# A convolution's stationary operand laid out by channel quartets, and half of x staged in VectorE's buffers

## The chip, the cores and the metric

The kernel runs on one core of one Trainium2 chip. The metric is the device time of one execution in microseconds (us). A core has a matrix engine (TensorE, "PE" in the profile; its weight loads are listed apart as "PEld"), VectorE ("DVE"), ScalarE ("ACT"), GpSimd ("POOL"), a queue engine ("SP") and 16 DMA engines. Each engine works through its own instruction queue in order and waits on semaphores for the others. On-chip tensors have 128 partitions; PS is the accumulation memory, eight banks of 128 x 512 numbers.

## The reference

Two independent halves, whose results lie side by side in the output. Half A is multi-head attention over 2048 positions with 32 heads of 16 channels. Half B is a gated long convolution over 512 channels:

```python
qkv = (x @ wqkv) ...                       # A: x is 2048 x 512
scores = einsum("bhqd,bhkd->bhqk", q, k) * Dh ** -0.5
a = (softmax(scores) @ v) @ wo
k_shift = sum of 4 shifted copies of k, each times shift_k[:, tap]     # B
kv = k_shift * v
y = causal convolution of kv with ssm_k (one filter of 2048 taps per channel) + kv * ssm_D
out = concatenate([a, q * y], -1)
```

## The kernel before, in words

*Attention.* x is transposed on TensorE (`turn_first` L663, `turn_x` L478) into xT; projections give KTo, QT and VAF. The scores come in blocks of 128 keys x 512 queries for one head (2048 blocks, L779, four heads side by side in row strips). Two or three blocks form a step T; ACT exponentiates two or three blocks in one instruction (L786, 726 of them) into PT. From step 82 on one block of many steps goes to DVE instead: a conversion of PS into the integer buffer EI (L805), a linear piece on GpSimd (L284), two polynomial steps (L814) and a last one into PTD (L815). 256 blocks go that way. Probabilities times values accumulate in PS (L854); DVE transposes and normalizes each finished group (L880 to L895); the output projection is L928 and L940.

*Convolution.* For half B, chunks of 256 positions of k (four shifted copies) and v are loaded; DVE multiplies and adds the taps (L588, L592) and multiplies by v into KV (L608, two instructions for each of eight chunks, `kv_chunk`). KV holds the gated values as [position in tile, time tile, channel], 16 tiles of 512 channels. The filters are written to memory reversed and read back, channel by channel, as Toeplitz tiles of 128 x 2048 into the ring WR (14 slots, `load_wr`, 512 loads of 512 KB on the SP queue). For each quartet of channels `conv_lags` (L980) runs 16 lags; lag n loads 16 - n columns of KV of one channel as weights and streams 128 columns of WR, four channels in four column strips of the array. A finished group of four quartets is copied by DVE (L996), transposed on PE (L1007), multiplied by q (L1022) and stored.

*KV is used twice.* Before the gated values exist, the 16 tiles of x are loaded into KV (`load_x`, L383) and transposed from there; each L608 waits for the semaphore of the transposes issued last (`h_xt`).

*Order.* A planner in the kernel's own code emits every engine's queue while the program is built. It keeps a clock for each engine from costs written beside each operation (460 ns for L608, 692 ns for most DVE operations); `dve_job` puts a DVE operation on a list with a due time, `commit_one` picks the next one, and PE's steps, convolution bursts (`emit_lags`), zero-weight filler matmuls (`keep_active`, L1104) and loads are placed by the same clock. A changed cost may thus change the order of everything behind it.

Of the kernel before, what the change touches and what calls it, by code (L numbers as in the profile page):

```python
# [6 lines left out]
ALU = mybir.AluOpType  # L7
BF16 = mybir.dt.bfloat16
# [16 lines left out]
C = 512  # L25
NB = S // 128
# [145 lines left out]
def bass_concat_heads__mha_block__ssm_conv_h3__prompt_kernel(  # L172
# [12 lines left out]
    x2, q2, k2, v2, out2 = A_x[0], B_q[0], B_k[0], B_v[0], out[0]  # L185
# [4 lines left out]
    def enter(cm):  # L190
        ctxs.append(cm)
        return cm.__enter__()
# [4 lines left out]
    def sb(name, shape, dt=BF16):  # L197
        return enter(nc.sbuf_tensor(name, shape, dt))
# [5 lines left out]
    VAF = sb("VAF", [128, KT, VROW])  # L204
    PT = sb("PT", [128, R_PT, 3 * QB])
    WR = sb("WR", [128, R_W, S])
    KV = sb("KV", [128, NB, C])
    QN = sb("QN", [128, NB, 256])
    WQ = sb("WQ", [128, 4, D])
    MSK = sb("MSK", [128, 2, 4], FP32)  # L210
# [7 lines left out]
    IDN = sb("IDN", [128, 128])  # L218
    SHK = sb("SHK", [128, 4, 4])
    PTD = sb("PTD", [128, 4, QB])  # L220
    EI = sb("EI", [128, 4, QB], INT32)
    EM = sb("EM", [128, 2, QB], FP32)
    ZER = sb("ZER", [128, 128])
    JNK = sb("JNK", [128, 2], FP32)
    WK = WKV[:, 0, :, :]
    WV = WKV[:, 1, :, :]
# [22 lines left out]
    def job(fn, deps, cost, due, then=None):  # L249
        j = Job(fn, deps, cost, due, then)  # L250
        jobs.append(j)
        return j
# [81 lines left out]
    def pe_op(fn, deps, mms):  # L334
        advance(pe.t)
        return pe.op(fn, [force(d) for d in deps], cost=Mm(*mms))

    def dve_op(fn, deps=(), cost=692.0):
        return dve.op(fn, [force(d) for d in deps], cost=cost)
# [3 lines left out]
    def dve_job(fn, deps, cost=692.0, slack=900.0, then=None, two=False):  # L343
        if dyn[0]:
            j = job(fn, deps, cost, pe.t + slack + cost, then)
            j.two = two
            return j
        h = dve_op(fn, deps, cost)
        if then:
            then(h)  # L350
        return h

    def full(n, k):
        return [("full", 0, n)] * k

    def dma(eng, dsem, outp, inp, deps=(), transpose=False):
        h = dsem.add()

        def fn(e):
            f = e.dma_start_transpose if transpose else e.dma_start  # L360
            f(outp, inp).then_inc(dsem.sem, 16)  # L361
        eng.op(fn, deps, inc=False)
        return h
# [16 lines left out]
    d_x0 = DmaSem(sem("d_xa"))  # L380

    def load_x(eng, ds, t0, t1):
        return dma(eng, ds, KV[:, t0:t1, :], x2[t0 * 128:t1 * 128, :].rearrange("(t p) d -> p t d", p=128))  # L383

    def landing(h, us):
        Eng.at[(id(h[0]), h[1])] = 1000.0 * us
# [52 lines left out]

    h_j = dve.op(lambda e: e.memset(JNK[:], 0.0))  # L440
    h_w0 = dve.op(lambda e: e.memset(PT[:, 0, 0:512], 0.0))
# [13 lines left out]
    h_vaf1 = pool.op(lambda e: e.memset(VAF[:, :, H * VW:VROW], 1.0))  # L455
    h_zer = pool.op(lambda e: e.memset(ZER[:, :], 0.0))
    h_kz0 = pool.op(lambda e: e.memset(KZS[:, :, S:S + PAD], 0.0))
# [3 lines left out]

    act.op(lambda e: e.activation(JNK[:, 1:2], JNK[:, 0:1], ACT.Exp), [h_j], inc=False)

# [4 lines left out]
    h_xt = [None]  # L468

    def turn_x(sc, cp, bank, eng):  # L470
        pbf = PS[:, bank, :].bitcast(BF16)

        def fn(e):
            ins = None
            for i in range(2):
                for t in range(4):
                    c = 2 * cp + i
                    ins = e.transpose(pbf[:, 512 * i + 128 * t:512 * i + 128 * t + 128],  # L478
                                      KV[:, 4 * sc + t, 128 * c:128 * c + 128], IDN[:, :])
            return ins  # L480
        h = pe_op(fn, [h_xn[sc], h_idn, bank_free[bank]], full(128, 8))
        h_xt[0] = h
        dst = xT[:, 2 * cp:2 * cp + 2, sc * 512:(sc + 1) * 512]
        src = pbf.rearrange("p (i s) -> p i s", i=2)
        if eng is act:
            hh = act.op(lambda e: e.activation(dst, src, ACT.Copy), [h], cost=940.0)
        else:
            hh = dve_job(lambda e: e.tensor_copy(dst, src), [h])
        bank_free[bank] = hh
        h_x.setdefault(sc, []).append(hh)  # L490
# [85 lines left out]
            evac_unit(u, bank, pe_unit(u, bank), eng)  # L576


    kv_pieces = []
    h_kvc = [None]  # L580

    def kv_chunk(j):
        b = kvbuf[kv_buf[j]]
        st = {}

        def tap(m):
            in1 = TB[:, m:m + 1, :].broadcast_to([128, 2, D])
            st[m] = dve_job(lambda e: e.tensor_tensor(b[m], b[m], in1, ALU.mult),  # L588
                            [h_kv[(j, 0)], h_kv[(j, 1)], h_tb[m]], 750.0, 3000.0)

        def add(m):
            st["a"] = dve_job(lambda e: e.tensor_tensor(b[3], b[3], b[m], ALU.add), [st[m], st[3], st.get("a")], 750.0, 3500.0)  # L592

        def last():
            def then(h):
                h_kvfree[j] = h
                nxt = {4: 1, 3: None, 2: 0}.get(j, j - 3)
                if nxt is not None and nxt >= 0:
                    load_kv(nxt)
                for d in {6: (0, 1), 5: (2, 3), 4: (4, 11), 3: (8, 9, 12, 13), 1: (5, 6, 7)}.get(j, ()):  # L600
                    load_wr(d, [h])
                if j == 5:
                    load_qn(0, [h_kzt[0]], 4, NB)
                    line[0] += 5000.0
                elif j == 0:
                    start_conv(h)
            for i in range(2):
                dve_job(lambda e, i=i: e.tensor_tensor(KV[:, NB - 1 - 2 * j - i, :], b[3][:, i, :], b[4][:, i, :], ALU.mult),  # L608
                        [st["a"], h_xt[0]], 460.0, 4000.0 + i, then if i else None)
        return [lambda m=m: tap(m) for m in (3, 2)] + [lambda: add(2), lambda: tap(1), lambda: add(1),  # L610
                                                       lambda: tap(0), lambda: add(0), last]

# [44 lines left out]
    def turn_first(cs, t0, dep):  # L657
        def fn(e):
            ins = None
            for c in cs:  # L660
                for t in range(t0, t0 + 2):
                    pbf = PS[:, first_bank[c], :].bitcast(BF16)
                    ins = e.transpose(pbf[:, 128 * t:128 * t + 128],  # L663
                                      KV[:, t, 128 * c:128 * c + 128], IDN[:, :])
            return ins
        return pe_op(fn, [dep, h_idn], full(128, 2 * len(cs)))

# [53 lines left out]
    def pvb(n):  # L721
        return BGB if n == 1 else PVB
# [246 lines left out]
    def conv_lags(qd, n0, n1):  # L969
        kk = qd % 8  # L970
        deps = [h_wr[4 * qd + c] for c in range(4)] + [h_kvc[0]]
        if kk % 4 == 0 and n0 == 0:
            deps.append(bank_free[BGB])

        def fn(e):
            ins = None
            for n in range(n0, n1):
                for c in range(4):
                    d = 4 * qd + c
                    ins = e.matmul(PS[32 * c:32 * c + NB - n, BGB, 128 * (kk % 4):128 * (kk % 4) + 128],  # L980
                                   lhsT=KV[:, n:NB, d],
                                   rhs=WR[:, d % R_W, 128 * (NB - 1 - n):128 * (NB - n)],
                                   start=(n == 0), stop=(n == NB - 1), tile_position=(0, 32 * c))
            return ins
        h = pe_op(fn, deps, [("col", c, 128) for n in range(n0, n1) for c in range(4)])
        if n1 == NB:
            for c in range(4):
                h_wrfree[4 * qd + c] = h
                if 4 * qd + c + R_W < C:
                    load_wr(4 * qd + c + R_W)  # L990
            if kk % 4 == 3:
                half = kk // 4
                src = PS[:, BGB, :]
                src = bass.AP(tensor=src.tensor, offset=PS[:, BGB, 127:128].offset,
                              ap=[src.ap[0], [128, 4], [-1, 128]])
                bank_free[BGB] = dve_job(lambda e: e.tensor_copy(YB[:, half, :].rearrange("p (k i) -> p k i", k=4), src),  # L996
                                         [h, (lambda: h_yb.get(qd // 8 - 1, WAIT)) if qd >= 8 else None])
                h_yb_in[qd // 4] = bank_free[BGB]
        return h
# [94 lines left out]
    def keep_active(T, limit):  # L1094
        n = open_group[0]
        for _ in range(3):
# [4 lines left out]
            def fn(e):  # L1101
                ins = None
                for s in range(4):
                    ins = e.matmul(PS[32 * s:32 * s + 32, pvb(n), :], lhsT=ZER[:, 0:32],  # L1104
                                   rhs=IDN[:, :].rearrange("p (a f) -> p a f", a=1).broadcast_to([128, 4, 128]),
# [61 lines left out]
    def keep_zero(e):  # L1167
        return e.matmul(PS[:, BGB, :], lhsT=ZER[:, :], rhs=IDN[:, :].rearrange("p (a f) -> p a f", a=1).broadcast_to([128, 4, 128]),
                        start=False, stop=False)
# [93 lines left out]
    while flow["NT"] is None or T < flow["NT"] + 2:  # L1263
# [12 lines left out]
        if T < T_DYN:  # L1276
            if early and early[0][0] <= T:
                t = max(max(Mm.tile), pe.t)
# [79 lines left out]
```

## Time and profile before

| | us |
|---|---|
| median of three runs | 864.66 (862.82 to 866.16) |
| the profiled execution | 861.98 |
| its span, first to last instruction | 860.2 |
| ScalarE busy | 835.9 |
| VectorE busy | 817.0 |
| TensorE busy | 726.8 |
| GpSimd busy | 295.2 |

A row of a group reads: line, engine, operation, output<-inputs, shape and count, then total busy time in us and the mean of one in ns, then the idle time of the engine just before these instructions and what ended it. A row of the waits reads: who waited <- for whom, us in total, times, longest. A row of a window gives the busy time of each engine in that stretch, with counts in brackets, TensorE's granted clock (1.00 is full), the DMA engines' busy share and GB/s. A row of the timeline gives start, duration, instruction and count, and in brackets the idle time ahead of it.

### The profile page before, as it was taken

How to read it: one execution, taken by the hardware profiler on the slowest of the kernel's cores; microseconds unless marked ns; L12 is line 12 of the kernel's file. 1: busy time of each engine (PE TensorE's matmuls, PEld its weight loads, DVE VectorE, ACT ScalarE, POOL GpSimd, SP SyncE). 2: the span in 40 equal slices, each digit the busy share in tenths (PEclk: the TensorE clock that was granted, in tenths of full speed). 3: DMA queues.
4: the chain of work that ended last, by engine and by line, in shares of the span. 5: the costliest groups of instructions: out<-in, count | busy, mean ns of one | idle time of the engine just before them, and what ended most of it. 6: DMA issues, size and time to landing. Idle time of an engine off the chain costs nothing.

```text
span 860.2 us, 30079 instructions
## 1 busy us (share of the span) xinstructions
PE 726.8 (84%) x13244; PEld 325.6 (38%) x13244; DVE 817.0 (95%) x1342; ACT 835.9 (97%) x732; POOL 295.2 (34%) x317
## 2 busy tenths in 40 slices
PE   8989988888788888888888888888888887888787
PEld 3322343434344434343434334343333333434332
DVE  3888999999999999999999999999999999999995
ACT  6999999999999999999999999999999999999997
POOL 3233132333333333333334433333333333333331
PEclk9999999999999999999999999999999999999999
DMA  9877599999999999999999999999999999999922
GB/s 314 300 242 261 168 362 330 367 402 380 372 369 354 406 363 386 380 370 377 369 350 366 345 393 403 387 376 372 374 377 327 349 386 393 377 366 393 383 88 74
DMA packets 88435, 295.69 MB, mean 344 GB/s; under 512 B 11125, under 2 KB 19314, under 8 KB 87922
## 3 DMA queue, kind: packets, MB, share of 16 engines
q1 hardware_dynamic: 82386, 280.00, 87.4%
q0 software_dynamic: 3776, 12.58, 4.3%
q8 instruction: 105, 1.72, 0.8%
q10 hardware_dynamic: 2144, 1.18, 0.5%
q14 instruction: 24, 0.20, 0.1%
HBM read 287.31 MB, written 6.42 MB: 341 GB/s over the span
## 4 chain that ended last, share of the span: by engine, by line
ACT 57%; DVE 30%; PE 10%; issue 2%; DMA 1%; POOL 0%; ACTq 0%; DVEq 0%
ACT PT L786 57%; DVE EM L814 6%; DVE PTD L815 6%; DVE EI L805 6%; DVE WKV L814 6%; PE PS L779 3%; PE PS L854 2%; PE PS L514 1%; PE PS L507 1%; DVE YB L996 1%; DMA WKV<-in_A_wqkv_dram 1%; PE PS L980 1%; DVE DT L880 1%; PE PS L500 1%; DVE OUTA L940 1%
## 5 line engine op out<-in xcount | busy, mean ns | idle before, releaser
L786 ACT ACTIVATE PT<-PS 128x1536 bf16<-128x1536 f32 (+1 forms) x726 | 832.3, 1362 | 12.8 <-PE PS L779 11.3
L779 PE MATMUL PS<-QT,KTo 32*128 32x512 bf16 x2048 | 285.5, 385 | 116.4 <-ACT PT L786 93.2
L980 PE MATMUL PS<-WR,KV 128*10 128x128 bf16 (+15 forms) x8192 | 255.9, 223 | 4.0 <-issue 2.7
L980 PEld LDWEIGHTS PS<-WR,KV 128*6 128x6 bf16 (+15 forms) x8192 | 184.5, 107 | 75.5 <-issue 41.7
L284 POOL TENSOR_SCALAR EM<-EI 128x512 f32<-128x512 uint16 x128 | 127.9, 999 | 224.1 <-DVE WKV L814 107.0
L284 POOL TENSOR_SCALAR WKV<-EI 128x512 f32<-128x512 uint16 x128 | 129.5, 1012 | 218.9 <-DVE EM L814 83.5
L854 PE MATMUL PS<-PT,VAF 128*32 128x512 bf16 x1792 | 186.3, 392 | 1.4 <-issue 0.5
L805 DVE TENSOR_SCALAR EI<-PS 128x512 int32<-128x512 f32 x256 | 182.2, 712 | 1.7 <-PE PS L779 1.3
L814 DVE SCALAR_TENSOR_TENSOR EM<-EM 128x512 f32<-128x512 f32 x256 | 181.0, 725 | 1.5 <-POOL EM L284 1.4
L814 DVE SCALAR_TENSOR_TENSOR WKV<-WKV 128x512 f32<-128x512 f32 x256 | 181.3, 727 | 0.9 <-POOL WKV L284 0.7
L779 PEld LDWEIGHTS PS<-QT,KTo 32*128 32x128 bf16 x2048 | 72.6, 91 | 271.8 <-ACT PT L786 222.1
L815 DVE SCALAR_TENSOR_TENSOR PTD<-EI,EM 128x512 uint16<-128x512 int32 x128 | 92.3, 722 | 0.4
L815 DVE SCALAR_TENSOR_TENSOR PTD<-EI,WKV 128x512 uint16<-128x512 int32 x128 | 91.5, 716 | 0.6
L854 PEld LDWEIGHTS PS<-PT,VAF 128*32 128x32 bf16 x1792 | 46.9, 93 | 105.5 <-issue 98.2
L854 PE MATMUL PS<-PTD,VAF 128*32 128x512 bf16 x256 | 78.3, 387 | 4.4 <-DVE PTD L815 3.8
L1104 PE MATMUL PS<-IDN,ZER 128*32 128x512 bf16 x440 | 46.7, 380 | 0.3 <-issue 0.3
L854 PEld LDWEIGHTS PS<-PTD,VAF 128*32 128x32 bf16 x256 | 19.6, 94 | 26.1 <-DVE PTD L815 17.4
L880 DVE STREAM_TRANSPOSE DT<-PS 128x512 f32<-128x512 f32 x31 | 23.6, 760 | 6.1 <-PE PS L854 5.8
L996 DVE CAST YB<-PS 128x512 bf16<-128x512 f32 x32 | 22.0, 687 | 0.2
L535 DVE TENSOR_TENSOR QT<-PS,MSK 128x1024 bf16<-128x1024 f32 x15 | 18.5, 1230 | 3.4 <-PE PS L500 3.3
L361 POOL DMA_DIRECT2D WR<-in_B_k_dram x15 | 11.0, 737 | 30.1 <-DVE KV L608 21.0
L361 POOL DMA_DIRECT2D out_dram<-OUTA x12 | 7.1, 590 | 38.2 <-DVE OUTA L940 38.2
(77 smaller groups left out, 312.8 us busy)
## 6 DMA issues: line engine op xcount, KB each, us to landing
WR<-kz_scratch SPq DMA_DIRECT2D x512, 512.0 KB, 7.7
WR<-in_B_k_dram POOLq DMA_DIRECT2D x15, 256.0 KB, 7.0
kz_scratch<-WR SPq DMA_DIRECT2D x1, 2176.0 KB, 8.6
out_dram<-QN POOLq DMA_DIRECT2D x2, 1024.0 KB, 8.5
QT<-in_B_k_dram POOLq DMA_DIRECT2D x7, 256.0 KB, 8.6
KV<-in_A_x_dram SPq DMA_DIRECT2D x3, 512.0 KB, 9.0
out_dram<-OUTA POOLq DMA_DIRECT2D x12, 128.0 KB, 5.6
WR<-in_B_v_dram SPq DMA_DIRECT2D x5, 256.0 KB, 4.8
```

What stands on the lines that cost most here:

```text
L284: q.h = pool.op(lambda e: e.tensor_scalar(UB[m % len(UB)], f, PA, PB, ALU.mult, ALU.add), [h, fx.h, free], cost=Beside((h[0], h[1] + 1)))
L535: hh = dve_job(lambda e: e.tensor_tensor(QT[:, qb % 2, 2 * o:2 * o + 2, :], src, MSK[:, :, 0:1].broadcast_to([128, 2, QB]), ALU.mult), [h, ...
L779: ins = e.matmul(PS[:, bank, :], lhsT=KTo[32 * s:32 * s + 32, g // 2, kt * 128:(kt + 1) * 128], rhs=QT[32 * s:32 * s + 32, qb % 2, g, :], ...
L786: h_exp[T] = act.op(lambda e: e.activation(PT[:, T % R_PT, 0:n * QB], PS[:, banks[0]:banks[0] + n, :].rearrange("p b f -> p (b f)"), ACT.E ...
L805: h_fix[i] = job(lambda e: e.tensor_scalar(ei, PS[:, bank, :], FIX_LO, FIX_ADD, ALU.max, ALU.add), [h, h_pair.get(i - 4)], 692.0, end)
L814: js.append(job(lambda e, c=c: e.scalar_tensor_tensor(u, u, c, u, ALU.add, ALU.mult), [js[-1]], 693.0, due + 700.0 * (len(js) - 3)))
L815: js.append(job(lambda e: e.scalar_tensor_tensor(PTD[:, i % 4, :].bitcast(UINT16), ei, 2.0 ** -9, u, ALU.mult, ALU.add), [js[2], (lambda: ...
L854: ins = e.matmul(PS[32 * s:32 * s + 32, pvb(qb * NG + g), :], lhsT=VAF[:, kt, h * VW:h * VW + 32], rhs=rhs, start=first[b], stop=last[b], ...
L880: h_t = dve_job(lambda e: e.transpose(out=dt, in_=PS[:, pvb(n), :]), [h, h_mult.get(n - 2 if n == 2 else n - 1) if n != 1 else None], 717. ...
L980: ins = e.matmul(PS[32 * c:32 * c + NB - n, BGB, 128 * (kk % 4):128 * (kk % 4) + 128], lhsT=KV[:, n:NB, d], rhs=WR[:, d % R_W, 128 * (NB - ...
L996: bank_free[BGB] = dve_job(lambda e: e.tensor_copy(YB[:, half, :].rearrange("p (k i) -> p k i", k=4), src), [h, (lambda: h_yb.get(qd // 8 ...
L1104: ins = e.matmul(PS[32 * s:32 * s + 32, pvb(n), :], lhsT=ZER[:, 0:32], rhs=IDN[:, :].rearrange("p (a f) -> p a f", a=1).broadcast_to([128, ...
```

## The change

KV is laid out as [position in tile, channel quartet, time tile, four channels]. A weight load of lag n then reads its 16 - n columns 4 elements (8 bytes) apart, where they were 512 elements (1,024 bytes) apart. The gated multiply writes 128 runs of four channels, 64 elements apart, where it wrote 512 channels in a row; its inputs are as before. A time tile of KV now lies across the whole buffer, so a gated tile would overwrite x everywhere: x keeps the first half of the buffer for its tiles 0 to 7 (XL, a flat view of KV), and its tiles 8 to 15 are loaded into EI, seen as bfloat16 (XH). The planner's cost of the multiply goes from 460 to 700 ns.

```diff
-    KV = sb("KV", [128, NB, C])
+    KV = sb("KV", [128, C // 4, NB, 4])
...
+    XL = KV[:, :, :, :].rearrange("p q t r -> p (q t r)").rearrange("p (t d) -> p t d", t=NB)
+    XH = EI[:, :, :].rearrange("p i f -> p (i f)").bitcast(BF16).rearrange("p (t d) -> p t d", t=8)
+
+    def xn(t):
+        return XL[:, t, :] if t < 8 else XH[:, t - 8, :]
...
     def load_x(eng, ds, t0, t1):
-        return dma(eng, ds, KV[:, t0:t1, :], x2[t0 * 128:t1 * 128, :].rearrange("(t p) d -> p t d", p=128))
+        return dma(eng, ds, XL[:, t0:t1, :] if t0 < 8 else XH[:, t0 - 8:t1 - 8, :], x2[t0 * 128:t1 * 128, :].rearrange("(t p) d -> p t d", p=128))
...
-                                      KV[:, 4 * sc + t, 128 * c:128 * c + 128], IDN[:, :])
+                                      xn(4 * sc + t)[:, 128 * c:128 * c + 128], IDN[:, :])
...
+    def quads(ap):
+        return ap.rearrange("p (q r) -> p q r", r=4)
+
...
-                dve_job(lambda e, i=i: e.tensor_tensor(KV[:, NB - 1 - 2 * j - i, :], b[3][:, i, :], b[4][:, i, :], ALU.mult),
-                        [st["a"], h_xt[0]], 460.0, 4000.0 + i, then if i else None)
+                dve_job(lambda e, i=i: e.tensor_tensor(KV[:, :, NB - 1 - 2 * j - i, :], quads(b[3][:, i, :]), quads(b[4][:, i, :]), ALU.mult),
+                        [st["a"], h_xt[0]], 700.0, 4000.0 + i, then if i else None)
...
-                                      KV[:, t, 128 * c:128 * c + 128], IDN[:, :])
+                                      xn(t)[:, 128 * c:128 * c + 128], IDN[:, :])
...
-                                   lhsT=KV[:, n:NB, d],
+                                   lhsT=KV[:, qd, n:NB, c],
```

## The prediction

> **What bounds the kernel now.** I read the page's busy times first, then the chain of work that ended last, then the groups with shapes kept apart, the waits, and two windows. ScalarE (ACT) and VectorE (DVE) are both nearly full:
>
> ```profile
> span 860.2 us, 30079 instructions
> PE 726.8 (84%) x13244; PEld 325.6 (38%) x13244; DVE 817.0 (95%) x1342; ACT 835.9 (97%) x732; POOL 295.2 (34%) x317
> ...
> ACT 57%; DVE 30%; PE 10%; issue 2%; DMA 1%; POOL 0%; ACTq 0%; DVEq 0%
> ```
>
> ```profile
> L786 ACT ACTIVATE PT<-PS 128x1536 bf16<-128x1536 f32 x340 | 528.0, 1608 | 5.0 <-PE PS L779 4.3
> L786 ACT ACTIVATE PT<-PS 128x1024 bf16<-128x1024 f32 x386 | 428.0, 1145 | 7.8 <-PE PS L779 7.1
> ```
>
> ```profile
> PEld PS L779 <- ACT PT L786: 222.1, 461, 1.2
> ACT PT L786 <- PE PS L779: 11.3, 25, 1.2
> SPq L361 <- PE PS L980: 294.4, 79, 7.5
> ```
>
> ```profile
> core 0: us, PE busy (x) PEld busy (x) DVE busy (x) ACT busy (x) POOL busy (x), PEclk, DMA share, GB/s
> 36.00:98.00 62.00, 56.18 (x370) 16.65 (x368) 54.90 (x96) 59.59 (x60) 15.86 (x20) 0.97 0.71 241
> 100.00:845.00 745.00, 625.78 (x12588) 292.39 (x12584) 732.84 (x1196) 736.96 (x631) 266.92 (x269) 1.00 0.97 361
> ```
>
> ACT runs the 726 exponentials almost without a break: 835.9 of 860.2 us, 24.3 us idle in all. Between 100 and 845 us, where the convolution runs, it is idle for 745.00 - 736.96 = 8.0 us and DVE for 12.2 us. The waits point one way: TensorE's loads for the scores stand 222.1 us behind ACT, while ACT stands 11.3 us behind TensorE (PE). So PE has room, ACT and DVE do not, and the queue that loads the Toeplitz tiles waits for PE to free them (294.4 us), not PE for it. Any change on PE alone can win at most those few microseconds of ACT's idle time.
>
> **The change, part by part.** The instruction order of both programs says that the counts stay: 740 instructions on ACT, 1344 on DVE, 544 on SP, 321 on POOL; 256 tiles are exponentiated on DVE in both. PE issues 12 filler matmuls fewer (428 for 440). Up to the first convolution lag PE's order is the same.
>
> *The gated multiply* (16 instructions) writes runs of four channels, 128 bytes apart, in place of 512 in a row. Its rows, and the nearest ones:
>
> ```profile
> L608 DVE TENSOR_TENSOR KV<-WR 128x512 bf16<-128x512 bf16 x10 | 3.8, 418 | 0.1
> L608 DVE TENSOR_TENSOR KV<-QT,QN 128x512 bf16<-128x512 bf16 x6 | 2.3, 417 | 0.0
> L1022 DVE TENSOR_TENSOR QN<-PS,QN 128x512 bf16<-128x512 bf16 x16 | 11.2, 700 | 0.2 <-PE PS L1007 0.2
> L551 DVE CAST VAF<-PS 128x512 bf16<-128x512 f32 x16 | 11.0, 690 | 8.1 <-PE PS L514 8.0
> L545 DVE CAST KTo<-PS 128x512 bf16<-128x512 f32 x15 | 10.5, 701 | 5.9 <-PE PS L507 5.8
> ```
>
> The low end is today's 418 ns; nothing in a scattered write can make it quicker. The high end is the multiply of the same size that runs at one element a cycle, L1022 at 700 ns: 16 x 282 ns = 4.5 us. L551 writes runs of 16 elements with gaps and takes 690 ns where the gapless L545 takes 701, so gaps in the output alone cost nothing there. I take 418 ns, that is 0, because the inputs stay contiguous and the runs stay of unit step; 0 to +4.5 us for the range. The Trainium skill ("VectorE: DVE Perf Modes", What auto-detection actually checks) says the same: a two-tensor operation keeps two elements a cycle if all tensors are 16-bit with step 1 inside, which the new output has; no run here shows it for runs of four. If it cost more, the cover is DVE's 62.00 - 54.90 = 7.1 us of idle time between 36 and 98 us.
>
> The code's planner is told 700 ns for it instead of 460. That reorders DVE's queue from its 60th instruction on, and moves the convolution's first lag from behind score block 191 to behind 194 of 2048, its last from 2009 to 2015. If the multiply really takes 418 ns, DVE runs 16 x 282 ns = 4.5 us ahead of its plan at 98 us, which can only shorten waits for it. ACT's idle time between 100 and 845 us that is not one of the two clock drops below (1.23 + 1.16) is 8.0 - 2.4 = 5.6 us; I credit a seventh, 0.8 us, since part of a lead is soon lost where DVE in turn waits for PE.
>
> *The weight loads of the convolution* read columns 8 bytes apart in place of 1,024:
>
> ```profile
> L980 PE MATMUL PS<-WR,KV 128*8 128x128 bf16 x512 | 40.7, 222 | 0.9 <-issue 0.9
> L980 PE MATMUL PS<-WR,KV 128*1 128x128 bf16 x512 | 39.0, 219 | 0.0
> L980 PEld LDWEIGHTS PS<-WR,KV 128*15 128x15 bf16 x512 | 26.2, 146 | 3.8 <-issue 0.9
> L980 PEld LDWEIGHTS PS<-WR,KV 128*1 128x1 bf16 x512 | 15.7, 83 | 6.1 <-issue 2.6
> L854 PEld LDWEIGHTS PS<-PT,VAF 128*32 128x32 bf16 x1792 | 46.9, 93 | 105.5 <-issue 98.2
> ```
>
> ```profile
> L980 PEld LDWEIGHTS PS<-WR,KV 128*6 128x6 bf16 (+15 forms) x8192 | 184.5, 107 | 75.5 <-issue 41.7
> ...
> L1104 PE MATMUL PS<-IDN,ZER 128*32 128x512 bf16 x440 | 46.7, 380 | 0.3 <-issue 0.3
> ```
>
> A load of 15 columns at the wide step takes 146 ns, one of 32 adjacent columns 93 ns. So the loads will shrink to 85 to 95 ns; from a mean of 107 that is some 15 ns for each of 8192. But the matmuls that they feed do not feel it: over the 16 forms, from 1 to 16 columns, 512 matmuls keep PE busy for 39.0 to 40.7 us (lowest and highest shown). All forms at the lowest would free at most 16 x 1.7 = 27 us of PE time, where PE stands 222.1 us behind ACT. I take 0; the range goes down to what ACT idles, 8.0 us. The Trainium skill ("SBUF — State Buffer", Door 1, the note on cachelines) has the reason for the shorter load: two hits on each 16-byte line are needed for full rate, and four bf16 channels at a step of 8 bytes give two. The trace agrees on the wide step (146 against 93 ns).
>
> *The staging of x.* Tiles 8 to 15 land in EI, the same two loads of 512 KB on the same queue:
>
> ```profile
> KV<-in_A_x_dram SPq DMA_DIRECT2D x3, 512.0 KB, 9.0
> ```
> ```profile
> L478 PE MATMUL PS<-IDN,KV x48: 219/219/230, 11.5 to 46.7; 128*128 128x128 bf16 x48
> ```
> ```profile
> 94.61 0.65 DVE L805 TENSOR_SCALAR EI<-PS 128x512 int32<-128x512 f32 x1
> ```
>
> The last transpose of x reads at 46.7 us, DVE's first conversion writes EI at 94.61 us: 48 us of cover, cost 0. No queue is given an instruction or a wait more.
>
> *The later end of the convolution.* Six score blocks are two exponentials:
>
> ```profile
> 813.37 24.21 ACT L786 ACTIVATE PT<-PS 128x1536 bf16<-128x1536 f32 x20
> ```
> ```profile
> 838.24 1.23 POOL L361 DMA_DIRECT2D out_dram<-QN  x1 [3.59 <-DVE QN L1022]
> ```
> ```profile
> out_dram<-QN POOLq DMA_DIRECT2D x2, 1024.0 KB, 8.5
> ```
> ```profile
> 853.84 0.72 DVE L880 STREAM_TRANSPOSE DT<-PS 128x512 f32<-128x512 f32 x1 [4.56 <-PE PS L854]
> ```
>
> 2 x 1.21 = 2.4 us later the last gate product and its store: the store lands near 838.2 + 8.5 + 2.4 = 849.1 us, 11 us before the end. DVE's last idle stretch of 4.56 us covers the shifted 1.4 us of its work. I take 0. The 12 fillers are 12 x 46.7 / 440 = 1.3 us of PE time, worth 0.
>
> *The sum:* 0 (multiply) - 0.8 (DVE early) + 0 (loads) + 0 (x) + 0 (tail). The profiled execution is 861.98 us (span 860.2 and 1.8 around it), so 861.2 for one like it; that execution lies 2.7 us under the median of the runs, 864.66, so the median goes to 863.9 us.
>
> **The rivals.**
>
> *Faster: PE's shorter loads take ACT's waits away.* ACT's waits are all for the scores (11.3 us, L779), and a convolution burst stands ahead of the scores in PE's queue. Against it: the matmul rows above. If every wait between 100 and 845 us went, the time is 864.66 - 8.0 = 856.7; it counts from half of that on, 860.3. By the Trainium skill ("TensorE: Matmul & The Clock Gate", Back-to-back issue gap) the spacing in a stream of loads and matmuls is set by both; were that so here, a form with 15 columns would be busier than one with 1 in the ratio of their loads, and 39.0 to 40.7 does not show it.
>
> *Slower: the multiply drops to one element a cycle.* Place: DVE between 36 and 98 us; price 282 ns x 16 = 4.5 us. It decides from 270 ns each on, if none of it lies in DVE's idle time, and then gives 864.66 + 4.5 = 869.2. For it: DVE is full from 100 us on, and 30% of the chain is its own. Against it: 7.1 us of cover, and the plan has reckoned with 700.
>
> *Slower: more half-speed stretches of TensorE's clock.* Three exponentials waited over 1 us, each at a stretch at half clock (first window: before it, second: in it):
>
> ```profile
> 78.01 2.96 ACT L786 ACTIVATE PT<-PS 128x1024 bf16<-128x1024 f32 x3 [1.17 <-PE PS L779]
> ```
> ```profile
> 135.59 2.38 ACT L786 ACTIVATE PT<-PS 128x1024 bf16<-128x1024 f32 x2 [1.23 <-PE PS L779]
> ```
> ```profile
> 445.47 1.47 ACT L786 ACTIVATE PT<-PS 128x1536 bf16<-128x1536 f32 x1 [1.16 <-PE PS L779]
> ```
> ```profile
> 439.60:443.00 3.40, 2.38 (x41) 1.02 (x38) 3.40 (x6) 3.40 (x4) 1.00 (x1) 1.00 0.98 382
> 443.00:446.40 3.40, 3.40 (x31) 1.08 (x32) 2.64 (x4) 2.24 (x3) 1.00 (x1) 0.50 0.93 335
> ```
>
> PE was busy 2.38 of 3.40 us ahead of it, below its mean of 2.86 (625.78 / 745 x 3.40). Shorter loads and 12 fillers fewer leave PE idler. Each drop costs ACT about 1.2 us; four more make 864.66 + 4.8 = 869.5. Fewer than three are as possible.
>
> **How the numbers follow.** A measurement of this kernel tells about 0.5% (4.3 us) from no change; its runs spread from 862.82 to 866.16. No visible change 0.45; faster by PE 0.25; slower by the multiply 0.20; slower by the clock 0.10. The low end is 864.66 - 5.6 = 859.0, all of ACT's waits without the clock drops; the high end is the full price of the multiply, 869.2. The likeliest case alone spans 860.3 to 869.0, 0.5% about the median.
>
> **What would show it.** Right: L608 near 418 ns, the L980 loads between 83 and 95 ns whatever their columns, the matmul forms unchanged near 39 us, ACT's busy time near 836 us and its idle time within 3 us of 24.3. Wrong: L608 near 700 with DVE's idle time gone between 36 and 98 us; more than five waits over 1 us ahead of L786; or ACT's idle time between 100 and 845 us cut to half, which would say that loads, not ACT, had paced the bursts.

## The result and the profile after

The changed kernel takes 853.78 us (median of 6 runs, 846.68 to 856.58), the kernel before 864.20 us (6 runs, 862.56 to 868.55). The ratio is 0.9857, with a 95% interval of 0.9808 to 0.9907: 1.4% faster. The forecast was 863.9 us, its low end 859.0.

The profiled execution of after took 848.04 us, with a span of 846.3 us, 13.9 us less than before. The page's first part and its groups, and the waits on both sides of the scores:

```profile
span 846.3 us, 30017 instructions
PE 710.1 (84%) x13188; PEld 308.1 (36%) x13232; DVE 799.7 (94%) x1342; ACT 820.7 (97%) x732; POOL 284.4 (34%) x317
...
L794 ACT ACTIVATE PT<-PS 128x1024 bf16<-128x1024 f32 (+1 forms) x726 | 817.2, 1348 | 13.8 <-PE PS L787 12.8
L988 PEld LDWEIGHTS PS<-WR,KV 128*1 128x1 bf16 (+15 forms) x8192 | 167.2, 87 | 84.3 <-issue 43.7
L289 POOL TENSOR_SCALAR WKV<-EI 128x512 f32<-128x512 uint16 x128 | 123.6, 965 | 221.1 <-DVE EM L822 85.6
L813 DVE TENSOR_SCALAR EI<-PS 128x512 int32<-128x512 f32 x256 | 173.5, 678 | 4.0 <-PE PS L787 3.8
L822 DVE SCALAR_TENSOR_TENSOR WKV<-WKV 128x512 f32<-128x512 f32 x256 | 171.0, 680 | 1.1 <-POOL WKV L289 0.7
```
```profile
PEld PS L787 <- ACT PT L794: 224.3, 468, 1.2
ACT PT L794 <- PE PS L787: 12.8, 30, 1.3
```

The gain is not where the forecast looked. ACT's idle time, 846.3 - 820.7 = 25.6 us, is 1.3 us *more* than before, and its waits for the scores went from 11.3 to 12.8 us. What fell is its busy time: from 835.9 to 820.7 us for the same 726 exponentials. DVE's fell from 817.0 to 799.7 us for the same 1342 instructions. These rows of the profile before, which the prediction didn't look at, carry the other half of the comparison:

```profile
L786 ACT ACTIVATE PT<-PS 128x1536 bf16<-128x1536 f32 (+1 forms) x726 | 832.3, 1362 | 12.8 <-PE PS L779 11.3
L284 POOL TENSOR_SCALAR WKV<-EI 128x512 f32<-128x512 uint16 x128 | 129.5, 1012 | 218.9 <-DVE EM L814 83.5
L805 DVE TENSOR_SCALAR EI<-PS 128x512 int32<-128x512 f32 x256 | 182.2, 712 | 1.7 <-PE PS L779 1.3
L814 DVE SCALAR_TENSOR_TENSOR WKV<-WKV 128x512 f32<-128x512 f32 x256 | 181.3, 727 | 0.9 <-POOL WKV L284 0.7
```

The same instruction on the same shape went from 712 to 678 ns (L805, now L813), from 727 to 680 ns (L814, now L822), and on GpSimd from 1012 to 965 ns. None of these lines was changed. The exponentials' busy time went from 832.3 to 817.2 us. Their mean, 1362 and 1348 ns, is of no use here: 726 x 1348 ns is 979 us, more than the span, so the recorded exponentials overlap, and the third experiment below has a mean of 1344 ns at 831.8 us of busy time.

The timeline of before shows what runs beside the long ones (start, duration, engine; TensorE's weight loads of the convolution and VectorE's polynomial steps in one stretch):

```profile
500.33 0.93 DVE L814 SCALAR_TENSOR_TENSOR WKV<-WKV 128x512 f32<-128x512 f32 x1
500.48 0.42 PEld L980 LDWEIGHTS PS<-WR,KV 128*16 128x16 bf16 x24 [0.23 <-issue]
...
503.04 0.42 PEld L980 LDWEIGHTS PS<-WR,KV 128*4 128x4 bf16 x16
503.14 0.68 DVE L814 SCALAR_TENSOR_TENSOR EM<-EM 128x512 f32<-128x512 f32 x1
```

The step that ran beside 24 loads of 16 to 11 columns took 0.93 us; the one beside 16 loads of 4 columns or fewer took 0.68. In the timeline of after, a step beside 16 loads of 15 columns and fewer takes 0.69:

```profile
301.54 0.22 PEld L988 LDWEIGHTS PS<-WR,KV 128*15 128x15 bf16 x16 [0.23 <-issue]
301.61 0.69 DVE L822 SCALAR_TENSOR_TENSOR EM<-EM 128x512 f32<-128x512 f32 x1
```

Over all 512 polynomial steps of before, I counted the weight columns that the convolution loads while each runs: without any the mean is 693 ns, with 200 or more 854 ns, and a straight line gives 0.54 ns for each column. After, the same count gives 683, 689 and 0.03 ns. That is a correlation inside a trace; the experiments ask for its cause.

### The profile page after: what moved, and what is told of

The parts are those of the page before. It is cut to its first block, busy times and chain, and to the rows that moved or that the text cites. A ratio compares the mean times of both kernels' runs of the same rounds, so it can differ in the third digit from the quotient of the medians.

```text
span 846.3 us, 30017 instructions
## 1 busy us (share of the span) xinstructions
PE 710.1 (84%) x13188; PEld 308.1 (36%) x13232; DVE 799.7 (94%) x1342; ACT 820.7 (97%) x732; POOL 284.4 (34%) x317
## 4 chain that ended last, share of the span: by engine, by line
ACT 62%; DVE 23%; PE 11%; issue 2%; DMA 1%; ACTq 0%
ACT PT L794 62%; DVE PTD L823 5%; DVE EI L813 5%; DVE EM L822 5%; PE PS L787 4%; DVE WKV L822 4%; PE PS L862 2%; PE PS L519 1%; DVE QT L540 1%; PE PS L988 1%; DMA WKV<-in_A_wqkv_dram 1%; DVE DT L888 1%; PE PS L505 1%; PE PS L512 1%; PE PS L936 1%
## 5 line engine op out<-in xcount | busy, mean ns | idle before, releaser
L794 ACT ACTIVATE PT<-PS 128x1024 bf16<-128x1024 f32 (+1 forms) x726 | 817.2, 1348 | 13.8 <-PE PS L787 12.8
L988 PE MATMUL PS<-WR,KV 128*8 128x128 bf16 (+15 forms) x8192 | 251.5, 220 | 4.4 <-issue 3.9
L988 PEld LDWEIGHTS PS<-WR,KV 128*1 128x1 bf16 (+15 forms) x8192 | 167.2, 87 | 84.3 <-issue 43.7
L289 POOL TENSOR_SCALAR WKV<-EI 128x512 f32<-128x512 uint16 x128 | 123.6, 965 | 221.1 <-DVE EM L822 85.6
L289 POOL TENSOR_SCALAR EM<-EI 128x512 f32<-128x512 uint16 x128 | 123.1, 962 | 219.4 <-DVE WKV L822 90.1
L813 DVE TENSOR_SCALAR EI<-PS 128x512 int32<-128x512 f32 x256 | 173.5, 678 | 4.0 <-PE PS L787 3.8
L822 DVE SCALAR_TENSOR_TENSOR WKV<-WKV 128x512 f32<-128x512 f32 x256 | 171.0, 680 | 1.1 <-POOL WKV L289 0.7
L822 DVE SCALAR_TENSOR_TENSOR EM<-EM 128x512 f32<-128x512 f32 x256 | 170.9, 686 | 0.2
L823 DVE SCALAR_TENSOR_TENSOR PTD<-EI,WKV 128x512 uint16<-128x512 int32 x128 | 87.2, 682 | 0.6
L823 DVE SCALAR_TENSOR_TENSOR PTD<-EI,EM 128x512 uint16<-128x512 int32 x128 | 86.9, 680 | 0.6
```

What stands on the lines that cost most here:

```text
L289: q.h = pool.op(lambda e: e.tensor_scalar(UB[m % len(UB)], f, PA, PB, ALU.mult, ALU.add), [h, fx.h, free], cost=Beside((h[0], h[1] + 1)))
L794: h_exp[T] = act.op(lambda e: e.activation(PT[:, T % R_PT, 0:n * QB], PS[:, banks[0]:banks[0] + n, :].rearrange("p b f -> p (b f)"), ACT.E ...
L813: h_fix[i] = job(lambda e: e.tensor_scalar(ei, PS[:, bank, :], FIX_LO, FIX_ADD, ALU.max, ALU.add), [h, h_pair.get(i - 4)], 692.0, end)
L822: js.append(job(lambda e, c=c: e.scalar_tensor_tensor(u, u, c, u, ALU.add, ALU.mult), [js[-1]], 693.0, due + 700.0 * (len(js) - 3)))
L823: js.append(job(lambda e: e.scalar_tensor_tensor(PTD[:, i % 4, :].bitcast(UINT16), ei, 2.0 ** -9, u, ALU.mult, ALU.add), [js[2], (lambda: ...
```

## The experiments

Two theories stood at the start. Theory A: weight loads whose columns lie 1,024 bytes apart lengthen what ScalarE, VectorE and GpSimd do at the same moment. Theory B: the reordered queues made the gain (the planner's cost of the multiply moved everything behind it). Each layout was also run with the other's order.

**The layout in the old order.** The changed kernel with

```diff
-                        [st["a"], h_xt[0]], 700.0, 4000.0 + i, then if i else None)
+                        [st["a"], h_xt[0]], 460.0, 4000.0 + i, then if i else None)
```

> The changed layout with the planner's cost of the multiply put back to 460 ns: every engine's queue then stands in the order of the kernel before, and only the layout (8-byte steps in the weight loads, runs of four in the multiply, x in EI) differs. Theory A (weight loads at a wide step lengthen what ScalarE, VectorE and GpSimd do at the same time): about 854 us, L805-type conversions near 680 ns and polynomial steps near 685 ns. Theory B (the new order of the queues made the gain): about 864 us. If both share it: between 856 and 861.

Measured: 849.67 us (4 runs, 844.04 to 855.56), ratio 0.9829 (0.9756 to 0.9901); L813 678 ns and the row of the polynomial step:

```profile
L822 DVE SCALAR_TENSOR_TENSOR WKV<-WKV 128x512 f32<-128x512 f32 x256 | 171.2, 683 | 0.9 <-POOL WKV L289 0.7
```

The layout alone makes the gain, all of it; the 854 us expected lies within its interval.

**The new order alone.** The kernel before with 460.0 made 700.0 in the same place.

> The layout of before with only the planner's cost of the multiply at 700 ns: the queues stand in the order of the changed kernel, the weight loads keep their step of 1,024 bytes. Theory A: 862 to 867 us, conversions near 712 ns and polynomial steps near 726 ns as before. Theory B: about 854 us.

Measured: 866.46 us (10 runs, 861.88 to 871.38), ratio 1.0029 (0.9994 to 1.0064).

```profile
L814 DVE SCALAR_TENSOR_TENSOR WKV<-WKV 128x512 f32<-128x512 f32 x256 | 178.3, 712 | 1.1 <-POOL WKV L284 0.7
```

Theory B falls: the order brings nothing; whether it costs a little the interval leaves open.

**Only the reading at the wide step.** Everything of the changed kernel, its order and its multiply included, with the step of the weight loads put back (XF is KV seen flat; d is the channel). The loads then pick other gated values than half B needs, in the same number and sizes:

```diff
-                                   lhsT=KV[:, qd, n:NB, c],
+                                   lhsT=XF[:, 8192 * (d // 512 % 1) + d % 512 + 512 * n:8192 * (d // 512 % 1) + d % 512 + 512 * (NB - 1) + 1:512],
```

> The changed kernel with one thing different: the weight loads of the convolution read their columns 1,024 bytes apart again out of the same buffer, so they pick other gated values than the reference's and half B comes out wrong; sizes, counts, order and the multiply are those of the changed kernel. Theory A: 862 to 866 us, with the load of 15 columns near 146 ns and VectorE's operations 5% longer. Theory B, or a gain from x in EI or from the multiply: about 854 us.

Measured: 867.11 us (10 runs, 861.88 to 873.09), ratio 1.0029 (0.9993 to 1.0065), the load of 15 columns 142 ns.

```profile
L824 DVE SCALAR_TENSOR_TENSOR WKV<-WKV 128x512 f32<-128x512 f32 x256 | 178.9, 714 | 1.1 <-POOL WKV L291 0.7
L796 ACT ACTIVATE PT<-PS 128x1024 bf16<-128x1024 f32 (+1 forms) x726 | 831.8, 1344 | 17.6 <-PE PS L789 16.2
```

The time is just above the 862 to 866 us expected. One operand's step takes the whole gain away: the exponentials are back at 831.8 us of busy time. The cause is the step of the weight reads, and neither the multiply nor where x waits.

**Which step.** The same line with s in place of 512 (`lhsT=XF[:, 16*s*(d // s % g) + d % s + s*n : ... : s]`, g groups of 16 s elements in the buffer), for 16, 64, 128 and 256 bytes, and with `d % 392 + 520 * n` for 1,040 bytes. Half B gets other gated values in these runs too.

> The changed kernel with the weight loads reading columns 16 bytes apart (other gated values than the reference's, so half B is wrong). Theory A1 (what costs is each separate 16-byte line that a load touches): as many lines as columns, so as slow as the step of 1,024 bytes, 862 to 866 us. Theory A2 (only wide steps hurt, because they fall on the same bank): close to the changed kernel, 852 to 857 us. The load of 15 columns: near 146 ns by A1, near 94 by A2.

> The changed kernel with the weight loads reading columns 64 bytes apart (other gated values, half B wrong). The step of 16 bytes left VectorE at 684 ns and the load of 15 columns at 109 ns; the step of 1,024 bytes gave 717 and 141. Where does the price begin? If it grows with the load's own duration: polynomial steps near 700 ns and a load of 15 columns near 125. If it begins only where columns fall on the same bank, at some wide power of two: 684 ns.

> As the run at 64 bytes, with columns 256 bytes apart (half B wrong). By a price that grows with the load's duration: between 700 and 717 ns for the polynomial step. By a bank of a wide power of two: either 684 ns or the full 717 ns, nothing in between.

> As the run at 1,024 bytes, with columns 1,040 bytes apart, so that no two fall at the same place of a wide power of two (half B wrong). If the distance itself or the number of lines is what costs: polynomial steps near 717 ns and the load of 15 columns near 141. If it is columns that fall on the same bank: near 684 ns and 109, as at 16 bytes, and a padded row would have done what the new layout does.

> As the run at 64 bytes, with the weight loads' columns 128 bytes apart (half B wrong): tells where the price begins, between 64 bytes (polynomial steps 686 ns, none) and 256 bytes (719 ns, all of it). If the bank repeats every 128 bytes: near 718 ns and 107 ns a load; if every 256: near 686 ns.

Measured, from the profile of each; the fourth column is the mean polynomial step beside 200 or more loaded columns, counted as above:

| step, bytes | mean load, ns | load of 15 columns | polynomial step beside 200 columns | ACT's exponentials, us busy | time, us (runs) |
|---|---|---|---|---|---|
| 8 (the change) | 87 | 94 | 689 | 817.2 | 853.78 (6) |
| 16 | 95 | 109 | 690 | 818.7 | 856.12 (4) |
| 64 | 95 | 111 | 693 | 817.7 | 851.73 (1) |
| 128 | 100 | 124 | 698 | 818.6 | 857.67 (1) |
| 1,040 | 95 | 109 | 701 | 817.3 | 850.47 (1) |
| 256 | 107 | 142 | 853 | 831.5 | 862.76 (1) |
| 1,024 | 107 | 142 | 846 | 831.8 | 867.11 (10) |

Four of the times are single runs; the argument rests on the columns before them.

The polynomial step's rows at 1,040, 128 and 256 bytes, in this order, one profile each:

```profile
L824 DVE SCALAR_TENSOR_TENSOR WKV<-WKV 128x512 f32<-128x512 f32 x256 | 171.8, 684 | 1.1 <-POOL WKV L291 0.7
```
```profile
L824 DVE SCALAR_TENSOR_TENSOR WKV<-WKV 128x512 f32<-128x512 f32 x256 | 172.4, 687 | 1.1 <-POOL WKV L291 0.7
```
```profile
L824 DVE SCALAR_TENSOR_TENSOR WKV<-WKV 128x512 f32<-128x512 f32 x256 | 179.3, 715 | 1.1 <-POOL WKV L291 0.7
```

The load itself grows in stages: 87 ns where two columns share 16 bytes, 95 where they don't, 100 at 128 bytes, 107 at 256. The load of 15 columns at 16 bytes, 109 ns, is neither of the two values expected (146 or 94). The price to the other engines has no such stages: next to none up to 128 bytes and all of it at 256 and 1,024. At 1,040 bytes, farther apart than any, it is gone, so the distance doesn't cost. At 16 bytes, where each column has 16 bytes of its own, there is none either, so the number of 16-byte lines doesn't cost. Of the seven steps tried, the two multiples of 256 bytes cost and the other five don't; 512 bytes was not run. That such columns fall on the same bank of the memory is the reading that fits; no run shows the bank itself.

One rival is left, the load's own duration, since the loads at 256 and 1,024 bytes are also the longest; being equally long at both, they don't decide between it and the step. The traces do, with each polynomial step sorted by the widest load that overlaps it in time. Before and in the runs at 256 and 1,024 bytes (the new order alone included), steps whose widest load has 9 to 12 columns average 715 to 725 ns, and the longest load beside them 120 to 122 ns; without any load they average 692 to 694. At 128 bytes, steps beside loads of 13 to 16 columns average 686 ns, against 688 without any, though the longest load beside them lasts 127 ns. Loads of that length cost at the one step and not at the other. The same count shows that the price is not even per column: beside loads of 8 columns or fewer alone the mean is 688 to 697 ns at the wide steps, little or nothing, and beside wider ones than 12 it is 768 to 795.

**A padded row.** If such steps are the whole cause, eight unused channels would do what the layout does. The kernel before with

```diff
-    KV = sb("KV", [128, NB, C])
+    KV = sb("KV", [128, NB, C + 8])
...
-        return dma(eng, ds, KV[:, t0:t1, :], x2[...])
+        return dma(eng, ds, KV[:, t0:t1, 0:C], x2[...])
...
-                dve_job(lambda e, i=i: e.tensor_tensor(KV[:, NB - 1 - 2 * j - i, :], ...
+                dve_job(lambda e, i=i: e.tensor_tensor(KV[:, NB - 1 - 2 * j - i, 0:C], ...
```

> The kernel before with eight unused channels at the end of each time tile of KV, so that the columns of a weight load lie 1,040 bytes apart; nothing else differs: x stays in KV, the multiply writes 512 channels in a row, the order and the planner's costs are those of before. If columns on the same bank are the whole cause: 846 to 856 us, polynomial steps near 685 ns, the load of 15 columns near 109 ns. If the new layout wins by anything else of its own (shorter loads of 94 ns, runs of four): 858 us or more.

Measured: 845.38 us (4 runs, 843.89 to 848.62), ratio 0.9775 (0.9707 to 0.9844), the load of 15 columns 110 ns.

```profile
span 842.2 us, 30034 instructions
PE 712.2 (85%) x13199; PEld 314.8 (37%) x13244; DVE 798.1 (95%) x1342; ACT 820.1 (97%) x732; POOL 285.6 (34%) x317
```
```profile
L814 DVE SCALAR_TENSOR_TENSOR WKV<-WKV 128x512 f32<-128x512 f32 x256 | 172.6, 690 | 0.9 <-POOL WKV L284 0.7
```

It is the lowest median of the study, just under the range expected, from 16 bytes a row, with no reordering and no staging of x in EI. Its interval overlaps with those of the change and of the first experiment, so that it beats them isn't shown. The shorter loads of the change (94 against 110 ns) win nothing that these runs show.

**The clock.** Runs of one kernel differ with the granted clock: before, 860.39 us at 0.992 and 869.64 at 0.982; the change, 846.68 at 0.994 and 855.71 at 0.980, some 0.6 to 0.9 us for each 0.001. Could more filler matmuls hold it up? The kernel of the first experiment with

```diff
-PACE = 350.0
+PACE = 342.0
...
-ACTIVE = 4800.0
+ACTIVE = 5600.0
```

> The changed layout in the order of before (849.7 us, clock 0.981 to 0.994) with the planner's threshold of TensorE activity at 5,600 in place of 4,800 and its pace of the convolution at 342 ns a lag in place of 350: 874 filler matmuls in place of 446. If the half-speed stretches of TensorE's clock still cost what they seem to (runs of one kernel are 0.8 us longer for each 0.001 of granted clock): clock 0.992 or more in all runs and 842 to 846 us. If the clock only goes along with the time, or the fillers get in the way of the scores: 850 us or more.

Measured: 855.60 us (8 runs, 852.95 to 860.36) at clocks of 0.984 to 0.995, ratio 0.9913 (0.9881 to 0.9946).

```profile
span 851.7 us, 30972 instructions
PE 740.7 (87%) x13680; PEld 317.0 (37%) x13680; DVE 803.2 (94%) x1346; ACT 822.1 (97%) x732; POOL 282.6 (33%) x318
```
```profile
ACT PT L794 <- PE PS L787: 16.9, 37, 2.0
```

Doubled fillers with the shorter pace do not keep the clock up, and they cost time: at 0.995 this kernel took 853.45 us, where the first experiment took 844.04 at 0.994. ACT's waits for the scores are 16.9 us here, 10.0 there. Since the pace was changed with the fillers, which of the two costs is open. Whether a lower clock lengthens the runs or only goes along with them stays open too, as the clock was not raised.

## Why the prediction was wrong

*What failed.* The step "any change on PE alone can win at most those few microseconds of ACT's idle time", and after it the sum's term "0 (loads)" and the range's low end, 864.66 less 5.6 us of ACT's waits. The step holds only if what ACT and DVE do takes as long as before. The weight loads were priced by what they cost PE and its matmuls, and there the working was nearly right: the forms' busy time after is 37.6 to 40.3 us, before 39.0 to 40.7, though a single matmul of the form with 16 columns went from 238 to 222 ns on average. What they cost the engines beside them was not priced at all. It measured 835.9 - 820.7 = 15.2 us of ACT's busy time and 17.3 us of DVE's. ACT's 15.2 us, less the 1.3 us that it idles more, are the 13.9 us of the span. The prediction's own sign for being right, ACT's busy time near 836 us, is the one that failed. Its rivals reached beyond its range (856.7 and 869.5 us), but none to 853.8.

*The trace of before had it.* The prediction quoted DVE conversions of 512 elements at 690 and 701 ns, mostly from before the convolution begins, as prices for the multiply. L805 and L814 at 712 and 727 ns stood in the same list. The spread of L814 on one shape, 626 to 1,130 ns for its steps on EM, would not have told: after the change it is 623 to 1,099. Sorted by what TensorE loads meanwhile, it tells: 693 ns beside no load and 854 beside 200 columns.

*The load's own duration.* The note that the prediction cites from the Trainium skill ("SBUF — State Buffer", Door 1, cachelines) explains it in part: 87 ns with two columns to 16 bytes, 95 with one. The further growth at 128 and 256 bytes, and the effect on other engines, are not in that note.

*Who slows whom.* The Trainium skill ("SBUF — State Buffer", Who interferes with whom) says that only the port pair shared by VectorE and GpSimd contends, and that PE and ACT never wait on anyone. Here it differs: 14 to 15 us of ACT's exponentials come and go with the step of PE's weight reads, and the measurement decides.

*What was right.* The multiply takes 418 and 420 ns at its medians, so runs of four keep the rate and the 4.5 us rival is out. The rule cited for it from the Trainium skill ("VectorE: DVE Perf Modes", What auto-detection actually checks) agrees. The loads came out at 82 to 94 ns (83 to 95 forecast). Staging x in EI costs nothing that a run shows. ACT's idle time is within the 3 us named.

*The credit for an early DVE* (0.8 us) is not borne out: the order alone gave 866.46 us against 864.26. *The rival of the clock* is not what happened: two exponentials of after waited over 1 us for the scores (1.02 and 1.30), three of before. Nor does the clock make the difference between the kernels. At a granted clock of 0.992 to 0.994, where both have runs, before takes 859.6 to 863.6 us (over all its sets of runs) and the change 846.7 to 848.0.

*The rival "PE's shorter loads take ACT's waits away"* ended on the right side for the wrong reason, which is luck: ACT's waits rose, from 11.3 to 12.8 us.

## What to carry to other kernels

A bound read from idle time holds only as long as the durations hold: before calling an engine's busy time fixed, compare one instruction's duration beside and away from the operation that changes. Where weight loads read many columns 256 or 1,024 bytes apart, as here, try padding the row by 16 bytes before rearranging anything. And when one edit also changes a planner's cost, run the layout and the cost apart.

## What the runs showed of the hardware

- TensorE's weight loads with columns 256 or 1,024 bytes apart lengthened VectorE's polynomial steps by 0.51 to 0.54 ns on average for each column loaded meanwhile (little or nothing beside loads of 8 columns or fewer: 688 to 697 ns, against 692 to 694 beside none). ScalarE's exponentials of three blocks grew by 0.31 to 0.34 ns for each column and GpSimd's linear pieces by 0.5 to 0.8 ns. At 8, 16, 64, 128 and 1,040 bytes the slope was 0.05 ns or less on VectorE's steps and 0.07 or less on these exponentials.
- GpSimd's pieces still show slopes of up to 0.24 ns at those other steps, and ScalarE's exponentials of two blocks 0.25 to 0.31 (0.43 to 0.62 at the wide ones), so for these two a part of the slope is not the step's.
- A load of 15 columns took 94 ns at a step of 8 bytes, 109 at 16 and 1,040 (110 in the padded kernel), 111 at 64, 124 at 128 and 142 at 256 and 1,024 in these runs (146 in the profile of before).
- A two-tensor multiply on VectorE that writes runs of four 16-bit elements 128 bytes apart took as long as one that writes them in a row (418 and 420 against 417 and 418 ns).
